# First batch of a fused attention and mixer kernel: the weights e turned in blocks by VectorE and moved by SP, and q and k of five pairs loaded by tokens and turned by TensorE

## The chip, the cores and the metric

The kernel runs on one core of one Trainium2 chip. The time is that of the device in microseconds (us), median of several executions. A profile is one execution, recorded by the hardware; its span is about 2 us shorter than the time. Where a ratio is given, it is the mean time of one kernel's fast runs over the mean of the fast runs of the kernel before in the same rounds on the same chip, so it is not quite the quotient of the medians beside it; the bracket is its 95% interval. The median of the kernel before drifted between 1377.9 and 1380.0 us from one sitting to the next, so small differences are read from the ratios, and two ratios whose intervals overlap are not told apart.

## The reference

```python
scores = q @ k.T / 8                      # 8 batches x 8 heads, 576 tokens, 64 per head
scores = where(scores >= max(scores) - tau, scores, -1e9)
attn   = softmax(scores) @ v              # -> x: 8 x 576 x 512
u      = x + (relu(x.T @ w_tok1) @ w_tok2).T
out    = u + relu(u @ w_ch1) @ w_ch2
```

All is float32; the mixer's weights come as float64 and are converted on the chip while the first two batches run.

## The kernel before

Work is cut into 144 units: a batch has four pairs of heads, two pairs are nine units of 128 query rows (both heads of a pair), so a batch is 18 units. A unit is scores (TensorE), maxima (VectorE), threshold and exponential (ScalarE), normalisation (GpSimd), and then e must be turned so that keys lie on partitions. Three units make a group, whose e is multiplied with v together ("the product"). From the second batch on, the mixer of the batch before runs in TensorE's gaps. The first batch has no such filling, but VectorE, ScalarE and GpSimd convert weights in it.

Each engine takes its instructions in the order in which the program issues them. In a round of the loop over u that order is: scores(u), the product that is due, norm(u-1), weight steps, the turning of unit u-2, weigh(u) (ScalarE), more weight steps, loads, the preparation of the next pair.

```python
def turn(u, third):                       # first batch: by TensorE
    ps = ps_tr.tile(...)                  # PSUM, two buffers, shared with the product
    for c in range(3):
        nc.tensor.transpose(out=ps[:, c, :], in_=e[:, k0 : k0 + P], identity=ident)
    on = nc.scalar.copy if third == 1 and u % 2 else nc.vector.tensor_copy
    on(out=eTs[key][...], in_=ps)

def turn_blocks(u):                       # later batches: 32x32 blocks by VectorE, then moves
    nc.vector.transpose(out=T[:, :, place, :]..., in_=e...)
    if place == GU - 1:                   # the group's last unit
        eT = work.tile([P, GU, 4, NK * 32], F32, tag="eT", bufs=1, name=f"eT_{u}")
        for a in range(4):
            for i in range(4):
                nc.sync.dma_start(out=eT[32*a : 32*a+32, :, i, :], in_=T[32*i : 32*i+32, a, :, :])

def prep(n):                              # q and k of a pair, loaded in 32-wide columns
    nc.vector.transpose(out=sb, in_=src...)   # once for q, once for k

# ...
for x, ps in xs:                          # after the product
    if in_blocks(b): nc.scalar.copy(out=x, in_=ps)
    else: copies.append(lambda x=x, ps=ps: nc.vector.tensor_copy(out=x, in_=ps))
# ...
due.append((u + (2 if in_blocks(wb) else 1), wb, wp, g))   # when the group's product is called
```

## Time and profile before

| | before |
|---|---|
| time | 1378.74 us, 3 runs (1378.43 to 1379.69) |
| span of the profile | 1375.1 us |
| first maxima of unit 0 / 8 / 17 / 18 | 9.4 / 49.0 / 99.8 / 106.2 us |
| x of the first batch starts to be turned ("tx") | 125.4 us |
| from tx to the end | 1249.7 us |

The first batch proper is units 0 to 17. Its x is complete at tx, two units into the second batch, and from there the mixer has work for TensorE. The lines of the profile are in the prediction.

### The profile page before, as it was taken

The page shows a single profiled execution, that of the slowest core. Times are in us where ns is not written, and L with a number is a line of the kernel's source. Part 1 is how long each engine was busy: PE and PEld are TensorE (multiplying, and loading weights), DVE is VectorE, ACT ScalarE, POOL GpSimd, SP SyncE. Part 2 cuts the span into 40 slices and gives each one's busy share as a digit, 9 for nine tenths or more (in the row PEclk, how much of TensorE's full clock was granted, in tenths as well). Part 3 has the DMA queues.
Part 4 walks back from the last instruction along what each step waited for, and adds up shares of the span by engine and source line. Part 5 has one row for each costly group of instructions (what it writes and reads, how often), then busy time and mean ns, then how long its engine had stood idle before and what let it go on. Part 6 is the DMA issues. An engine that isn't in the chain of part 4 may idle for free.

```text
span 1375.1 us, 17691 instructions
## 1 busy us (share of the span) xinstructions
PE 1322.7 (96%) x6226; PEld 817.9 (59%) x6226; DVE 588.2 (43%) x1017; ACT 581.8 (42%) x1288; POOL 356.0 (26%) x683
## 2 busy tenths in 40 slices
PE   6877799999999999999999999999999999999998
PEld 3444465646565666565665567565656576575675
DVE  6788875445444443434244444434333453201000
ACT  5666654454445444443434444353333444120110
POOL 4555653222222222222122222222121222100000
PEclk9988999999999999999999999999999999999999
DMA  5434655454544354433344435434433442400000
GB/s 121 98 96 125 183 142 124 100 123 98 122 109 114 82 121 94 113 88 95 77 100 94 113 77 123 106 83 98 103 87 75 107 103 63 115 1 16 8 11 21
DMA packets 278871, 128.20 MB, mean 93 GB/s; under 512 B 200896, under 2 KB 271552, under 8 KB 278784
## 3 DMA queue, kind: packets, MB, share of 16 engines
q1 hardware_dynamic: 150176, 111.06, 32.0%
q10 hardware_dynamic: 128608, 16.01, 7.3%
q8 instruction: 50, 0.82, 0.3%
q14 instruction: 37, 0.30, 0.1%
HBM read 43.25 MB, written 9.44 MB: 38 GB/s over the span
## 4 chain that ended last, share of the span: by engine, by line
PE 85%; DVE 7%; DMA 2%; SPq 2%; ACT 1%; issue 1%; POOL 1%; ACTq 0%; DVEq 0%; POOLq 0%
PE c L486 26%; PE c L470 26%; PE sc L302 11%; PE pv L413 9%; PE t L441 5%; PE t L448 3%; PE pv L408 3%; DVE mx L307 2%; SPq L374 2%; PE tx L432 1%; PE c L482 1%; DMA eT<-T 1%; PE tr L353 1%; DVE wc L205 1%; ACT e L317 1%
## 5 line engine op out<-in xcount | busy, mean ns | idle before, releaser
L307 DVE TENSOR_REDUCE mx<-sc 128x1 f32<-128x576 f32 x288 | 204.5, 751 | 487.9 <-PE sc L302 487.5
L470 PE MATMUL c<-xT,wc 128*128 128x256 f32 (+1 forms) x1920 | 399.4, 362 | 2.1 <-DVE xT L452 1.2
L486 PE MATMUL c<-wc,g 128*128 128x512 f32 x864 | 390.5, 597 | 0.0
L470 PEld LDWEIGHTS c<-xT,wc 128*128 128x128 f32 x1920 | 334.5, 191 | 71.5 <-issue 27.6
L308 POOL TENSOR_SCALAR bias<-mx,toff 128x1 f32<-128x1 f32 x288 | 82.8, 288 | 799.3 <-DVE mx L307 742.3
L317 ACT ACTIVATE e<-sc,bias 128x576 f32<-128x576 f32 x288 | 199.6, 739 | 162.0 <-POOL bias L308 161.4
L486 PEld LDWEIGHTS c<-wc,g 128*128 128x128 f32 x864 | 157.8, 190 | 175.7 <-issue 174.0
L471 ACT ACTIVATE g<-c 128x256 f32<-128x256 f32 (+1 forms) x240 | 86.7, 362 | 334.1 <-PE c L470 317.9
L324 ACT ACTIVATE e<-e,ntau 128x576 f32<-128x576 f32 x288 | 220.7, 771 | 0.0
L335 POOL TENSOR_SCALAR e<-e,rr 128x576 f32<-128x576 f32 x288 | 215.6, 761 | 15.8 <-DVE rr L332 4.3
L302 PE MATMUL sc<-kT,qT 64*128 64x288 f32 (+1 forms) x1280 | 196.6, 447 | 11.1 <-DVE kT L284 7.1
L365 DVE STREAM_TRANSPOSE T<-e 128x1152 f32<-128x1152 f32 x126 | 172.1, 1366 | 6.3 <-DMA eT<-T 2.6
L302 PEld LDWEIGHTS sc<-kT,qT 64*128 64x128 f32 (+1 forms) x1280 | 107.4, 184 | 98.3 <-issue 59.1
L413 PE MATMUL pv<-eT,lv 128*64 128x384 f32 (+1 forms) x1024 | 136.8, 409 | 0.0
L413 PEld LDWEIGHTS pv<-eT,lv 128*64 128x64 f32 x1024 | 76.1, 138 | 51.0 <-issue 43.6
L491 DVE COPY o<-c 128x512 f32<-128x512 f32 x36 | 24.9, 692 | 177.5 <-PE c L486 177.5
L418 ACT COPY xT<-pv 128x384 f32<-128x384 f32 (+1 forms) x56 | 21.0, 401 | 157.5 <-PE pv L413 157.5
L448 PE MATMUL t<-w,a 128*128 128x288 f32 x256 | 75.2, 421 | 7.2 <-DVE xT L452 5.3
L441 PE MATMUL t<-x_sb,w 128*128 128x512 f32 x160 | 72.1, 598 | 0.0
L448 PEld LDWEIGHTS t<-w,a 128*128 128x128 f32 x256 | 45.6, 191 | 32.2 <-issue 11.4
L452 DVE TENSOR_TENSOR xT<-xT,t 128x288 f32<-128x288 f32 x64 | 28.2, 446 | 80.5 <-PE t L448 80.0
L324 ACT ACTIVATION_READ_ACCUMULATOR e<-e,ntau 128x1 f32 x288 | 56.5, 196 | 0.0
(44 smaller groups left out, 554.7 us busy)
## 6 DMA issues: line engine op xcount, KB each, us to landing
eT<-T SPq DMA_DIRECT2D x672, 108.0 KB, 2.2
scratch<-in_moe_w_ch_dram SPq DMA_DIRECT2D x24, 512.0 KB, 3.7
lv<-in_v_dram SPq DMA_DIRECT2D x32, 288.0 KB, 3.3
out_dram<-o SPq DMA_DIRECT2D x36, 256.0 KB, 2.2
lk<-in_k_dram ACTq DMA_DIRECT2D x111, 72.0 KB, 2.6
lq<-in_q_dram ACTq DMA_DIRECT2D x106, 72.0 KB, 2.3
lq<-in_q_dram SPq DMA_DIRECT2D x22, 72.0 KB, 3.2
lk<-in_k_dram SPq DMA_DIRECT2D x17, 72.0 KB, 3.3
```

The costliest lines, as they stand in the source:

```text
L302: nc.tensor.matmul(sc[h][rows, f, 0:HS], lhsT=qT[r, cols], rhs=kT[r, HS * f : HS * f + HS], start=True, stop=True)
L307: nc.vector.tensor_reduce(out=mx[:, c], in_=sc[h][:, :, 0:HS], axis=AX.XY, op=ALU.max)
L317: nc.scalar.activation(out=eh, in_=sc[h][:, :, 0:HS], func=AF.Prelu, bias=bias[:, h : h + 1], scale=SCALE, alpha=STEEP)
L324: nc.scalar.activation(out=eh, in_=eh, func=AF.Exp, bias=ntau, accum_out=rs[:, h : h + 1])
L335: nc.gpsimd.tensor_scalar(out=eh, in0=eh, scalar1=rr[:, h : h + 1], scalar2=1.0, op0=ALU.mult, op1=ALU.mult)
L365: nc.vector.transpose(out=T[:, :, place, :].rearrange("p a (c x) -> p c a x", c=NK), in_=e.rearrange("p (c a x) -> p c a x", c=NK, a=4))
L413: nc.tensor.matmul(to[r], lhsT=lv[:, j, :], rhs=e[j], start=False, stop=(c == NI - 1), skip_group_check=True)
L441: nc.tensor.matmul(ps, lhsT=w1[:, t, P * m : P * m + P], rhs=x_sb[:, t, :], start=(t == 0), stop=(t == NT - 1))
L448: nc.tensor.matmul(ps, lhsT=s["a"][:, m, P * c : P * c + P], rhs=w2[:, m, HS * f : HS * f + HS], start=(m == 0), stop=(m == NTK - 1))
L470: nc.tensor.matmul(ps, lhsT=wc1[:, j, c, :], rhs=uT[:, c, GR * i : GR * i + n], start=(c == 0), stop=(c == NCC - 1))
L471: nc.scalar.activation(out=s["g"][:, j, 0:n], in_=ps, func=AF.Relu)
L486: nc.tensor.matmul(flat, lhsT=s["g"][:, j, P * t : P * t + P], rhs=wc2[:, j, :], start=False, stop=(j == NJ - 1), skip_group_check=True)
```

## The change

Its intent, as the code shows it: take TensorE's turns, whose PSUM tiles must be emptied by VectorE, out of the first batch, as the later batches already do, and lighten the loads of q and k. It has four parts:

1. Units 0 to 14 are turned in blocks by VectorE and moved by 16 DMAs a group on SP's queue into the one tile eT; the last group (units 15 to 17) is turned by TensorE as before.
2. The product of such a group is called three units after its last turn, not one.
3. The first batch's products are copied from PSUM by ScalarE, not VectorE.
4. q and k of pairs 0 to 4 are loaded with tokens on partitions (256-byte packets, six loads a pair) and turned by TensorE through two PSUM tiles, in place of eight loads of 128-byte packets and a block turn by VectorE.

```diff
+    NATURAL = NP + 1
+    def load_natural(n, eng):
+        for src, t, on in zip((q, k), loaded[n], eng):
+            for h in range(2):
+                on.dma_start(out=t[:, 0:NI, h, :], in_=src[b, 2*p + h, 0:MAIN, :].rearrange("(c t) d -> t c d", t=P))
+            on.dma_start(out=t[0:LAST, NI, :, :], in_=src[b, 2*p : 2*p + 2, MAIN:S, :].rearrange("h t d -> t h d"))
...
-    def in_blocks(b):
-        return b > 0
+    def in_blocks(b, p0, g):
+        return (b, p0, g) != (0, NP - 2, 2)
     def prep(n):
...
-            nc.vector.transpose(out=sb, in_=src.rearrange("p n d -> p (n d)"))
+            for lo, hi in ((0, NI), (NI, NT)):
+                ps = ps_tr.tile([P, MAIN], F32, tag="tr", name=f"{name}{lo}_{n}")
+                for c in range(lo, hi):
+                    nc.tensor.transpose(out=ps[...], in_=src[0:M, c]..., identity=ident[0:M, 0:M])
+                nc.vector.tensor_copy(out=sb[:, P*lo : min(P*hi, S)], in_=ps[...])
...
     # in weigh(u), between threshold and exponential
+        while copies:
+            copies.popleft()()
...
-                copies.append(lambda x=x, ps=ps: nc.vector.tensor_copy(out=x, in_=ps))
+                copies.append(lambda x=x, ps=ps: nc.scalar.copy(out=x, in_=ps))
...
-                due.append((u + (2 if in_blocks(wb) else 1), wb, wp, g))
+                due.append((u + (1 if not blocks else 2 if wb else 3), wb, wp, g))
```

More of the change, by code (lines that the diff above doesn't have):

```diff
@@ L100, in load_qk @@
         if n not in loaded:
-            loaded[n] = [ld.tile([P, S // 32, 32], F32, tag=tag, bufs=1, name=f"{tag}_{n}") for tag in ("lq", "lk")]
+            loaded[n] = [ld.tile([P, NT * 2 * D], F32, tag=tag, bufs=1, name=f"{tag}_{n}")[:, 0:S].rearrange("p (n d) -> p n d", d=32) for tag in ("lq", "lk")]
         for part in parts:
@@ L115, in load_v @@
         vals[n] = lv
+    NATURAL = NP + 1
+    def load_natural(n, eng):
+        b, p = pairs[n]
+        loaded[n] = [ld.tile([P, NT, 2, D], F32, tag=tag, bufs=1, name=f"{tag}_{n}") for tag in ("lq", "lk")]
+        for src, t, on in zip((q, k), loaded[n], eng):
+            for h in range(2):
+                on.dma_start(out=t[:, 0:NI, h, :], in_=src[b, 2 * p + h, 0:MAIN, :].rearrange("(c t) d -> t c d", t=P))
+            on.dma_start(out=t[0:LAST, NI, :, :], in_=src[b, 2 * p : 2 * p + 2, MAIN:S, :].rearrange("h t d -> t h d"))
     vals = {}
@@ L121 @@
         nc.gpsimd.memset(t, 0.0)
-    load_qk(0, (nc.sync, nc.scalar))
+    load_natural(0, (nc.sync, nc.scalar))
     w1 = const.tile([P, NT, DTOK], F32, name="w1")
@@ L283, in prep @@
             sb = work.tile([P, S], F32, tag=name, name=f"{name}_{n}")
-            nc.vector.transpose(out=sb, in_=src.rearrange("p n d -> p (n d)"))
             made.append(sb)
+            if n >= NATURAL:
+                nc.vector.transpose(out=sb, in_=src.rearrange("p n d -> p (n d)"))
+                continue
+            for lo, hi in ((0, NI), (NI, NT)):
+                ps = ps_tr.tile([P, MAIN], F32, tag="tr", name=f"{name}{lo}_{n}")
+                for c in range(lo, hi):
+                    M = MT[c]
+                    nc.tensor.transpose(
+                        out=ps[:, P * (c - lo) : P * (c - lo) + M], in_=src[0:M, c].rearrange("t h d -> t (h d)"), identity=ident[0:M, 0:M]
+                    )
+                nc.vector.tensor_copy(out=sb[:, P * lo : min(P * hi, S)], in_=ps[:, 0 : min(P * hi, S) - P * lo])
         heads[n] = made
@@ L400, in values @@
             ps = whole[:, first : first + N]
-            if in_blocks(b):
+            if in_blocks(b, p0, g):
                 to, e = ps.rearrange("p (m x) -> p m x", x=32), eT[:, first // 32 : (first + N) // 32]
@@ L416, in values @@
         for x, ps in xs:
-            if in_blocks(b):
+            if b:
                 nc.scalar.copy(out=x, in_=ps)
             else:
-                copies.append(lambda x=x, ps=ps: nc.vector.tensor_copy(out=x, in_=ps))
+                copies.append(lambda x=x, ps=ps: nc.scalar.copy(out=x, in_=ps))
     def token_mlp(b):
@@ L541, in values_due @@
             if p0 == NP - 2 and g == 2:
-                if not in_blocks(b):
+                if not b:
                     return True
@@ L560 @@
         last = False
-        if due and not in_blocks(due[0][1]):
+        if due and not due[0][1]:
             last = values_due(u)
@@ L569 @@
             weight_to(2.25 * (u - 1.5))
-        while copies:
-            copies.popleft()()
         if last:
+            while copies:
+                copies.popleft()()
             push(0)
@@ L575 @@
             wb, wp, wt = units[w]
-            if not in_blocks(wb):
+            blocks = in_blocks(wb, wp, wt // GU)
+            if not blocks:
                 for i in range(3):
@@ L582 @@
                     split_middle(wb * NP + wp + g)
-                due.append((u + (2 if in_blocks(wb) else 1), wb, wp, g))
+                due.append((u + (1 if not blocks else 2 if wb else 3), wb, wp, g))
         if b_now:
             fill(0.4)
-        if back and in_blocks(wb):
+        if back and blocks:
             turn_blocks(w)
@@ L605 @@
             if u == 0:
-                load_qk(1, (nc.sync, nc.sync), range(0, 3))
+                load_natural(1, (nc.sync, nc.sync))
             if t in when:
                 m, lo, hi = when[t]
-                if n + m < len(pairs):
+                if n + m < NATURAL:
+                    if lo == 0:
+                        load_natural(n + m, (nc.sync, nc.sync))
+                elif n + m < len(pairs):
                     load_qk(n + m, (nc.scalar if b_now else nc.sync,) * 2, range(lo, hi))
@@ L616 @@
                 prep(n + 2)
-        if due and in_blocks(due[0][1]):
+        if due and due[0][1]:
             values_due(u)
```

## The prediction

> **What bounds the kernel now.** I read the page first: its slices, then its chain, then the busy time of each engine by stage, and at last the order of instructions inside the first batch, the only stage that the change touches. (The program runs 144 units of attention, 18 to a batch; below "unit 8" is the ninth, and a "group" is three units whose turned weights e are multiplied with v together.)
>
> ```profile
> PE   6877799999999999999999999999999999999998
> DVE  6788875445444443434244444434333453201000
> PEclk9988999999999999999999999999999999999999
> ...
> core 0: us, PE busy (x) PEld busy (x) DVE busy (x) ACT busy (x) POOL busy (x), PEclk, DMA share, GB/s
> 7.00:106.20 99.20, 80.80 (x452) 48.77 (x452) 76.89 (x163) 65.66 (x137) 53.48 (x89) 0.91 0.43 99
> 106.20:126.50 20.30, 13.93 (x59) 7.74 (x58) 18.29 (x34) 13.68 (x29) 12.80 (x15) 0.66 0.61 157
> 126.50:200.00 73.50, 62.34 (x302) 40.41 (x303) 63.98 (x95) 46.41 (x97) 44.42 (x51) 0.98 0.58 155
> 200.00:1200.00 1000.00, 994.35 (x4743) 607.45 (x4742) 417.75 (x709) 433.08 (x971) 243.26 (x518) 1.00 0.44 101
> ```
>
> From 200 us on TensorE is busy 99.4% of the time; nothing in the change touches that work. The first batch is 7 to 126 us. No engine is full there: in 7 to 106.2 TensorE has 80.8, VectorE 76.9, ScalarE 65.7 of 99.2 us. So it is bound by engines that wait for each other. The chain of waits says how:
>
> ```profile
> 61.41 2.03 PE sc L302 x8
> 63.45 1.48 PE pv L408 x4
> 64.92 2.71 PE pv L413 x16
> 67.66 0.57 DVE xT L420
> 68.27 1.03 PE tr L353 x6
> ...
> 72.98 0.17 DVE rr L332
> 73.14 0.59 DVE wc L205
> 73.73 0.48 DVE eT L355
> 74.25 0.55 PE tr L353 x3
> 74.80 1.76 PE sc L302 x16
> ```
>
> TensorE turns three blocks, waits for VectorE to empty PSUM, turns the next three, and only then gets to the next scores; VectorE, in its own order, waits for the product with v (67.66) before it can copy it. The groups of VectorE in 7 to 106.2 us size the waits (last columns: idle time before them):
>
> ```profile
> L307 DVE TENSOR_REDUCE mx<-sc 128x1 f32<-128x576 f32 x37 | 26.3, 745 | 8.7 <-PE sc L302 8.4 <-issue 0.2
> L355 DVE COPY eT<-tr 128x384 f32<-128x384 f32 x40 | 21.1, 552 | 4.5 <-PE tr L353 4.5
> L420 DVE COPY xT<-pv 128x384 f32<-128x384 f32 x3 | 1.7, 558 | 6.9 <-PE pv L413 6.9
> L420 DVE COPY xT<-pv 128x192 f32<-128x192 f32 x4 | 1.2, 351 | 0.8 <-PE pv L413 0.8
> ```
>
> Of VectorE's 22.3 us idle, 12.2 (4.5 + 6.9 + 0.8) belong to the turning on TensorE and the copy of the product; about 7 of the 8.4 for scores are start-up, before unit 3. Later batches already move e as the change does in the first, and give its price:
>
> ```profile
> 180.48 10.38 SPq L374 DMA_DIRECT2D eT<-T  x16
> ...
> L365 DVE STREAM_TRANSPOSE T<-e 128x1152 f32<-128x1152 f32 x126 | 172.1, 1366 | 6.3 <-DMA eT<-T 2.6
> ...
> eT<-T SPq DMA_DIRECT2D x672, 108.0 KB, 2.2
> ```
>
> One turn of a unit is 1.37 us of VectorE; the 16 moves of a group are 10.4 us of SP's queue, and the last lands some 2.2 us after its issue.
>
> **What the Trainium skill says.** "VectorE: DVE Perf Modes", The three transpose paths: VectorE turns only 32x32 blocks, a full 128x128 turn is TensorE's and lands in PSUM. Agrees: the block turn has its 16 moves behind it, TensorE's has a copy of 0.55 us per three blocks. "DMA: Bandwidth & Descriptors", Anatomy of one DMA: about 2 us fixed, mostly the receipt of the last byte, and semaphore waits are held by the issuing sequencer, so one waiting DMA holds up all behind it on SP. The landing of 2.2 us agrees; the trace of before shows SP waiting for VectorE's T. "TensorE: Matmul & The Clock Gate", What's actually happening: after an idle window of about 3.4 us the array runs at half clock. Agrees: a unit's scores take 1.17 us in the dense part and 2.0 to 2.3 after pauses (61.41 above), granted clock 0.66 in 106 to 126. "SBUF — State Buffer", Who interferes with whom: two-input VectorE operations and GpSimd reads lock each other out; the weight step of 0.68 us takes up to 1.68 beside GpSimd's. It stays as it is.
>
> **The change part by part.**
>
> 1. Turning of units 0 to 14. VectorE loses 2.5 copies x 0.55 = 1.38 us a unit (ScalarE had one of six), gains one turn of 1.37: nothing. TensorE loses 15 x 9 = 135 turns, about 1.7 us a unit, and the ping-pong with them. ScalarE loses 0.24 a unit. Gain on VectorE's waits: 4.5 us at most.
>
> 2. Copies of the product from VectorE to ScalarE: VectorE loses 1.7 + 1.2 = 2.9 us of work in the window and the 7.7 us of waits. ScalarE, at 66%, takes them at 0.4 to 0.5 us each.
>
> 3. Preparing pairs 0 to 4. Before: two turns, 0.77 + 0.74 = 1.5 us of VectorE. After: ten turns on TensorE and four copies. A PSUM copy of 512 is 0.69 us (the output copy's row), one of 64 about 0.2 (estimate), so 1.78 us of VectorE, +0.28 a pair. Worse is the order: two PSUM tiles, so k's turns wait for q's copies. With four turns at 0.15 us plus 0.1: 0.7 turn, 0.75 copy, 0.7 turn, then 0.7 + 0.2 of copies or the next scores: 3.15 us where TensorE and VectorE take turns. In return a pair's eight loads of 576 packets of 128 B (4608) become six loads with 2304 packets of 256 B: they should land earlier at the start, perhaps by 1.5 us (estimate; the first landed at 5.6 to 5.8 us). Net for pair 0: +0.9 us. Pair 1 at unit 2: +1.6. So unit 4's first maximum, at 26.8 us before, comes at 29.3.
>
> 4. SP. 16 moves x 0.65 = 10.3 us a group, on a queue that had almost nothing to do; plus weights, v and q/k, about 14 us per group. It fits, narrowly.
>
> The new chain in the first batch: there is one buffer eT. A group's moves can't start before the group before has been multiplied. So a round is: 15 issues x 0.65 + 2.2 to the last landing = 12.0 us; product 4.2 us (1.48 + 2.71 above; TensorE comes from a pause, so cold); 0.1 of signalling: **16.3 us** for three units. Before, units 7 to 16 started at 44.0 and 93.1: 49.1 us for nine, 16.4 for three. The new bound is as long as the old one.
>
> Worked through in time: first turned group complete 3.7 us into unit 4, at 33.0 us; moves land 45.0; product ends 49.2; the preparation of pair 2 follows in TensorE's order (+3.15), so unit 8 starts at 52.4 (before 49.0: +3.4). Three rounds later the fourth product ends at 49.2 + 48.9 = 98.1, the preparation of pair 4 follows, unit 17 starts at 101.3 (before 99.8: +1.4). Unit 17 took 6.4 us and loses the wait for the product (0.8), its copies (0.6): 5.0, so unit 18 starts at 106.2, as before. The fifth product ends 114.4, inside unit 18 or 19, which are bound by weights on VectorE (8.5 us each) and unchanged. The last copy on ScalarE need not stand behind VectorE's weights: -0.5. Sum: **-0.5 us**. From there on the program is the same and the shift arrives at the end one to one.
>
> **The rivals.**
>
> A. The waits go and nothing takes their place: VectorE sets the pace. It would save 12.2 us of waits plus 2.9 of work, less 4 x 0.28 of copies and 2.5 at the start: about -11 us, 1368. For: later batches do it so without trouble. Against: their groups have some 27 us (product at 219.05 and 240.87, then 262), those of the first only 16, so the one eT has slack there and not here.
>
> B. The single eT and SP are tighter than I count: a q/k load or a weight piece between the moves (SP stood up to 2.5 us on one load at the start), a move slower with the queues full. Each microsecond costs five times, +5 to +10 us: 1384 to 1389. Against: fewer packets for q and k, and the two units of slack before each preparation.
>
> C. The cold clock: with its turns gone, TensorE pauses longer and scores take 2.3 us. Off the path while VectorE is behind; after each product half of a unit's scores counts, about +0.6 us five times: +3.
>
> D. TensorE's total falls by 135 - 50 = 85 turns. Worth nothing, since it isn't full there.
>
> **Range and chances.** My count gives 1378; the change is visibly fitted to the schedule (the wait of three units, the last group left as it was), so I give A about a third: point **1376**, range **1365 to 1385**. 2% is 27.6 us. All waits of VectorE in the window together are 22.3 us, so faster by 2% is next to impossible (0.02); slower would need five rounds longer by over 5 us each (0.02); within 2% 0.96.
>
> **What would show it.** Right: in 7 to 106 us VectorE's waits for TensorE's turns gone, but new ones before the maxima, behind the product with v; TensorE idle before the product, released by the move of T to eT; the moves waiting for the product; rounds near 16 us; maxima of unit 8 later than 49.0, of unit 18 within 3 us of 106.2; granted clock below 0.91; from 200 us on the same. Wrong: unit 18 at 96 or sooner with VectorE over 85% busy (A), or rounds over 18 us with SP without a gap (B). Also wrong if the saved time were lost again between 126 and 200 us, where weights and SP set the pace.

## The result

| | before | after |
|---|---|---|
| time | 1379.42 us, 6 runs | 1392.82 us, 6 runs (1392.35 to 1394.80) |
| ratio | | 1.0096 (1.0082 to 1.0109) |
| first maxima of unit 0 | 9.4 | 10.8 |
| unit 4 | 26.8 | 30.5 |
| unit 8 | 49.0 | 58.4 |
| unit 17 | 99.8 | 113.8 |
| unit 18 | 106.2 | 119.4 |
| tx | 125.4 | 141.5 |
| from tx to the end of the profile | 1249.7 | 1251.4 |

The change costs 13.4 us, about 1%. The two profiles lie 17.8 us apart, more than the medians: that of before is of an execution of 1376.9 us, faster than any timed one, that of after of the slowest, 1394.8.

The slices and the busy times by stage after, with the same columns as before:

```profile
PE   7667899999999999999999999999999999999998
...
7.00:106.20 99.20, 71.88 (x271) 40.70 (x271) 70.07 (x128) 60.16 (x125) 51.55 (x83) 0.86 0.63 159
119.40:140.00 20.60, 14.71 (x80) 8.73 (x82) 17.87 (x33) 11.74 (x24) 12.76 (x15) 0.75 0.78 198
140.00:215.00 75.00, 64.50 (x306) 40.84 (x304) 62.87 (x91) 45.69 (x92) 44.70 (x50) 0.95 0.57 151
215.00:1215.00 1000.00, 994.82 (x4746) 607.19 (x4743) 419.10 (x710) 435.37 (x977) 245.68 (x519) 1.00 0.43 100
```

(The granted clock of 0.86 from 7 to 106 us, and the 0.91 of before, are too high: the record of the clock begins only at 54.5 us in this profile, at 24.1 in that of before, and the table counts what is not recorded as full clock. The last section comes back to this.)

In the same 99.2 us every compute engine did less than before: VectorE 70.1 us in place of 76.9, ScalarE 60.2 in place of 65.7. So no engine became the bound; the engines wait longer for each other. Only the DMA engines are busier, 0.63 in place of 0.43. The dense part from 215 us on is as it was. What VectorE waited for from 7 to 119 us, before (first fence) and after (columns: who waited for whom, us in total, times, longest; the stretch is the same, but the changed kernel is one unit behind in it):

```profile
DVE mx L307 <- PE sc L302: 8.4, 8, 2.4
DVE xT L420 <- PE pv L413: 7.7, 4, 2.9
DVE eT L355 <- PE tr L353: 6.0, 14, 1.0
```

```profile
DVE mx L329 <- PE sc L324: 16.4, 11, 3.8
DVE qT L307 <- PE qT L304: 13.4, 2, 8.8
DVE kT L307 <- PE kT L304: 4.5, 5, 1.1
```

The two waits that the change aimed at (the product, the turns) are gone, 13.7 us; 34.3 us stand where 22.1 stood. The chain of waits after shows the new loop (start, us, what):

```profile
46.28 2.23 DMA eT<-T
48.51 0.30 issue
48.81 1.55 PE pv L431 x4
50.36 4.70 PE pv L436 x16
55.06 0.60 PE qT L304 x4
...
84.20 2.32 DMA eT<-T
86.52 0.24 issue
86.76 1.54 PE pv L431 x4
88.30 4.52 PE pv L436 x16
92.84 0.64 SPq L397
```

Read it downwards: the last of 16 moves lands, the product runs, behind it in TensorE's order comes the preparation of a pair, and at 92.84, the moment the product ends, SP issues the next group's first move, which had been held back by the one eT. The moves themselves, on SP's queue, with the loads between them (start, us, how many):

```profile
73.27 11.54 SPq L397 DMA_DIRECT2D eT<-T  x16
84.92 0.52 SPq L188 DMA_DIRECT2D scratch<-in_moe_w_ch_dram  x1
85.53 1.06 SPq L126 DMA_DIRECT2D lq<-in_q_dram  x2
86.65 0.65 SPq L127 DMA_DIRECT2D lq<-in_q_dram  x1
87.40 1.09 SPq L126 DMA_DIRECT2D lk<-in_k_dram  x2
88.53 0.64 SPq L127 DMA_DIRECT2D lk<-in_k_dram  x1
```

The products start at 48.8, 67.5, 86.8 and 105.0 us: rounds of 18.7, 19.2 and 18.2 us for three units, where the kernel before took 16.4.

### The profile page after: what moved, and what is told of

Its sections match the earlier page's. It is cut to its first block, busy times and chain, and to the rows that moved or that the text cites. A ratio compares the mean times of both kernels' runs of the same rounds, so it can differ in the third digit from the quotient of the medians.

```text
span 1392.9 us, 17563 instructions
## 1 busy us (share of the span) xinstructions
PE 1332.4 (96%) x6141; PEld 819.3 (59%) x6141; DVE 588.0 (42%) x996; ACT 583.2 (42%) x1289; POOL 361.3 (26%) x683
## 4 chain that ended last, share of the span: by engine, by line
PE 86%; DVE 5%; SPq 3%; DMA 3%; ACT 1%; issue 1%; POOL 0%; ACTq 0%; DVEq 0%; POOLq 0%
PE c L509 27%; PE c L493 25%; PE sc L324 11%; PE pv L436 9%; PE t L464 5%; PE t L471 3%; SPq L397 3%; PE pv L431 3%; DVE mx L329 2%; PE tx L455 1%; PE c L505 1%; DMA scratch<-in_moe_w_ch_dram 1%; DMA eT<-T 1%; ACT e L339 1%; DVE T L388 1%
## 5 line engine op out<-in xcount | busy, mean ns | idle before, releaser
L493 PEld LDWEIGHTS c<-xT,wc 128*128 128x128 f32 x1920 | 333.9, 190 | 71.9 <-issue 27.6
L324 PE MATMUL sc<-kT,qT 64*128 64x288 f32 (+1 forms) x1280 | 210.0, 456 | 14.7 <-ACT e L339 14.2
L388 DVE STREAM_TRANSPOSE T<-e 128x1152 f32<-128x1152 f32 x141 | 192.7, 1367 | 6.6 <-DMA eT<-T 3.4
L324 PEld LDWEIGHTS sc<-kT,qT 64*128 64x128 f32 (+1 forms) x1280 | 115.2, 188 | 110.3 <-issue 60.8
L436 PE MATMUL pv<-eT,lv 128*64 128x384 f32 (+1 forms) x1024 | 143.4, 424 | 0.0
L436 PEld LDWEIGHTS pv<-eT,lv 128*64 128x64 f32 x1024 | 79.6, 144 | 54.8 <-issue 48.3
L431 PE MATMUL pv<-eT,vl 128*64 128x384 f32 (+1 forms) x256 | 48.2, 455 | 13.4 <-DMA eT<-T 12.0
```

The lines of the kernel that those rows point to most:

```text
L324: nc.tensor.matmul(sc[h][rows, f, 0:HS], lhsT=qT[r, cols], rhs=kT[r, HS * f : HS * f + HS], start=True, stop=True)
L388: nc.vector.transpose(out=T[:, :, place, :].rearrange("p a (c x) -> p c a x", c=NK), in_=e.rearrange("p (c a x) -> p c a x", c=NK, a=4))
L431: nc.tensor.matmul(to[r], lhsT=vl[:, r], rhs=e[NI], start=True, stop=False, skip_group_check=True)
L436: nc.tensor.matmul(to[r], lhsT=lv[:, j, :], rhs=e[j], start=False, stop=(c == NI - 1), skip_group_check=True)
L493: nc.tensor.matmul(ps, lhsT=wc1[:, j, c, :], rhs=uT[:, c, GR * i : GR * i + n], start=(c == 0), stop=(c == NCC - 1))
```

## The experiments

Each is an edit of the changed kernel unless it says "the kernel before". Fifteen were run. One gives a wrong result (no loads of pairs 2 to 4, under "Is it the loads?"); all others were correct.

### One part of the change at a time

**Only the copies on ScalarE** (the kernel before with part 3).

```diff
-                copies.append(lambda x=x, ps=ps: nc.vector.tensor_copy(out=x, in_=ps))
+                copies.append(lambda x=x, ps=ps: nc.scalar.copy(out=x, in_=ps))
```

> The kernel before with only the third part of the change: the copies of the first batch's product go from VectorE to ScalarE. If VectorE's wait for the product (7.7 us) and its copies (2.9 us) are on the path: -5 us or better, near 1374. Rival, the wait only moves on to the scores that stand behind the turns in TensorE's order: within 2 us of 1379.4.

Measured: 1379.79 us, ratio 1.0003 (0.9977 to 1.0030). The rival's number holds: 7.7 us of waits for the product were worth nothing. They moved on, but to the turns more than to the scores: in this run's profile VectorE waits 17.3 us for TensorE's turns (6.0 before) and 9.9 for scores (8.4 before), from 7 to 119 us (its tx starts at 129.6 us, 4.2 later than in the profile of before, though the times agree). A wait that another takes over is not a gain.

**Only q and k by tokens** (the kernel before with part 4).

```diff
-    load_qk(0, (nc.sync, nc.scalar))
+    load_natural(0, (nc.sync, nc.scalar))     # and so for pairs 1 to 4; prep() through TensorE for them
```

> The kernel before with only the second part of the change: q and k of five pairs loaded by tokens and turned by TensorE; e turned by TensorE as before. If every preparation costs by its exchange between TensorE and VectorE: +3.7 us until unit 3 and about +1.9 us for each of the other three, +9 us, near 1388. If the preparations cost only at the start: +3.7, near 1383. If the lighter loads were worth something: 1379 or less.

Measured: 1391.72 us, ratio 1.0085 (1.0057 to 1.0112). By the median dearer than any of the three expectations, but the first of them (9 us, a ratio of 1.0065) lies inside the interval. It is the same as the whole change within the intervals. The start and pair 1 cost 5.0 us (unit 4 at 31.8 us), pair 2 with the unit behind it another 4.2 (unit 9 is 9.2 late), pair 3 hardly anything (unit 16 is 9.8 late), pair 4 with the unit behind it 4.1 (unit 18 is 13.9 late). VectorE waits for TensorE's turns of q and k (6.8 us in all), and the scores and products behind them in TensorE's order come later (13.1 and 10.4 us of waits, 8.4 and 7.7 before).

**All but q and k by tokens** (part 4 undone).

```diff
-    NATURAL = NP + 1
+    NATURAL = 0                                # loads and preparation of all pairs as before
```

> The changed kernel with q and k of all pairs loaded and turned as before (VectorE's block turn), only e moved by SP. Theory of the serial round: the round of moves and product does not contain the preparation, so rounds stay at 18 to 19 us, and only the start (unit 4 earlier by 3.7 us) and the last preparation behind a product (3.3 us before unit 17) are won: -7 us, near 1386. Rival 1, each of the four preparations is fully on the path: -12 us, near 1381. Rival 2, the fine packets of 128 B and two more issues a pair hold up SP and the moves: no gain, 1391 or more.

Measured: 1391.92 us, ratio 1.0093 (1.0063 to 1.0123). The start was won as expected (unit 4 at 27.6 us, not 30.5), and unit 8 came 7.7 us sooner than in the changed kernel, but at the preparation of pair 3 all was lost again: the eight fine loads stood on SP's queue, some before and the last two behind the third group's moves (69.1 to 79.4 us).

```profile
81.65 0.78 DVE L298 STREAM_TRANSPOSE qT<-lq 128x576 f32<-128x576 f32 x1 [9.02 <-issue]
83.02 0.78 DVE L298 STREAM_TRANSPOSE kT<-lk 128x576 f32<-128x576 f32 x1 [0.59 <-DMA lk<-in_k_dram]
```

The bracket is VectorE's idle time before the instruction: 9.0 us. The view names no releaser for it ("issue"), but the trace has the last load of q landing at 81.57 us, just before the turn starts. So parts 1 and 4 belong together in this schedule: with the moves on SP, the old loads come too late; with the new loads, the preparations cost TensorE and VectorE an exchange. The costs don't add: each half alone is as slow as the whole.

### The loops: one buffer, and three units of lag

**Two buffers eT** (the second lies in the tile of the channel mixer, unused in this batch).

```diff
-            eT = work.tile([P, GU, 4, NK * 32], F32, tag="eT", bufs=1, ...)
+            eT = work.tile([P, GU, 4, NK * 32], F32, tag="g" if b == 0 and (u // GU) % 2 else "eT", bufs=1, ...)
```

> The changed kernel with two buffers eT in the first batch (the second lies in a tile that is not used there). Theory, one eT makes a serial round of moves (12 us) plus cold product (5.4 to 6.3 us): with two buffers the moves start when VectorE has turned the group, rounds of products fall from 18.2-19.2 us to about 15 (then TensorE's order and SP's 14 us bind), unit 17 starts some 9 us earlier, total near 1384. Rival, SP's queue is full anyway (moves plus loads of q, k, v and weights): rounds stay over 18 us and the total over 1390.

Measured: 1392.55 us, ratio 1.0104 (1.0077 to 1.0130): no gain, and my theory that the one eT alone sets the round fell. The second group's moves did start at 48.7 us, not at 55.1, but the products still started at 49.4, 66.2, 84.3 and 103.0 us. TensorE stands before them all the same where the moves come late, as here before the fourth:

```profile
102.97 1.55 PE L431 MATMUL pv<-eT,vl 128*64 128x384 f32 x4 [3.65 <-DMA eT<-T]
104.28 5.09 PE L436 MATMUL pv<-eT,lv 128*64 128x384 f32 x16
```

The second theory: two loops of like length. One goes through eT. The other goes through the lag: turn, moves, product, and behind the product in TensorE's order the next scores, which feed the next turns. With three units of lag and some 4.3 us a unit there are 13 us for moves of 12 and a product of 5 to 6.

**Lag of four units, one eT**, and **lag of four units, two eT**. (The fifth group keeps three, so as not to delay the end of the batch.)

```diff
-                due.append((u + (1 if not blocks else 2 if wb else 3), wb, wp, g))
+                due.append((u + (1 if not blocks else 2 if wb else 3 if wp and g == 1 else 4), wb, wp, g))
```

> The changed kernel with the product called four units after a group's last turn, not three (the fifth group keeps three); one eT. Two eT alone gave nothing: products still came 16.8 to 18.7 us apart. Theory: two loops of like length run side by side, the one through the single eT (moves 12 us, product 6) and the one through TensorE's order (turn, moves, product, then the scores behind it, three units on). A longer lag opens only the second: the products stay over 17.5 us apart and the total within 3 us of 1392.8. Rival, the lag alone is what is too short: total 1387 or less.

> Two eT and four units of lag, so both loops open. Theory: TensorE no longer stands before its products, VectorE's waits of 9 us at unit 7 and 5 us at unit 16 shrink to the preparations' own 3 us, unit 18 comes near 110 us, total near 1383. Rival, SP and the loads are the limit (moves start late behind loads): total stays over 1389.

Measured: 1390.32 us, ratio 1.0085 (1.0057 to 1.0113), and 1384.97 us, ratio 1.0045 (1.0023 to 1.0068).

| | lag three | lag four |
|---|---|---|
| one eT | 1392.8 | 1390.3 |
| two eT | 1392.6 | 1385.0 |

Either alone wins 0 to 2.5 us, both win 7.8; by the ratios it is -1 to 1.5 and 7. Only the gain of both is clear of the intervals. That is what two loops side by side look like. The products' lines say the same; with one eT TensorE still waits for the moves (2.69 us before the third product), with two it doesn't:

```profile
86.97 1.55 PE L431 MATMUL pv<-eT,vl 128*64 128x384 f32 x4 [2.69 <-DMA eT<-T]
88.27 4.58 PE L436 MATMUL pv<-eT,lv 128*64 128x384 f32 x16
```

```profile
82.54 1.55 PE L431 MATMUL pv<-eT,vl 128*64 128x384 f32 x4
83.87 4.24 PE L436 MATMUL pv<-eT,lv 128*64 128x384 f32 x16
```

### Is it the loads?

In the version with both loops open the moves of the groups began 12.6, 17.9, 18.3 and 12.5 us apart, and the two long distances are those with loads of q and k between. So I took SP's issues for the limit that was left.

**Loads of pairs 2 to 4 issued by ScalarE**, in the changed kernel and with both loops open.

```diff
-                        load_natural(n + m, (nc.sync, nc.sync))
+                        load_natural(n + m, (nc.scalar, nc.scalar))
```

> The changed kernel (one eT, lag three) with the loads of q and k of pairs 2 to 4 issued by ScalarE, not SP. In the trace SP issues 10.4 us of moves and then 6 to 8 us of loads in a round of 18. If SP's issues alone set the round, it falls to 13-15 us and the total to 1385 or less. If the loop through the one eT (12 us of moves, 6 of cold product) is as long as SP's, the products stay 17.5 to 18.5 us apart and only the 2 us before the first move are won: 1389 to 1392.

> As before with two eT and four units of lag, but the loads of q and k of pairs 2 to 4 issued by ScalarE. With both loops open SP was the limit that was left: its moves began 12.6 us apart where no loads lay between and 17.9 and 18.3 us where they did. Theory: with the loads away the moves follow VectorE's turns, 13 to 15 us apart, and the total falls from 1385 to about 1380; what is left to 1378 is the preparations by TensorE. Rival: nothing is won, 1384 or more.

Measured: 1396.58 us, ratio 1.0126 (1.0102 to 1.0151), and 1389.52 us, ratio 1.0070 (1.0050 to 1.0090). Both are slower than with the loads on SP (ratios 1.0096 and 1.0045), by 3 to 4 us; each interval overlaps that of its partner, so it is the two together, and the traces, that speak for a loss. The moves of the third group, in the changed kernel 11.5 us (above), took, with the loads on the other queue:

```profile
73.95 17.32 SPq L397 DMA_DIRECT2D eT<-T  x16
```

SP's queue stood, as its own waits show, until a load of q landed, though ScalarE had issued it (8.0 us in two waits, the longest 5.2):

```profile
SPq L397 <- DMA lq<-in_q_dram: 8.0, 2, 5.2
```

Why should a move of e wait for a load of q? The trace shows the semaphores: in this run all DMAs, of both queues, tell of their landing through the same eight (numbers 100 to 107), used again and again, and a DMA waits until the one that used its semaphore before has landed. The move at 89.33 us waits for number 102, whose last user was a load of q that ScalarE issued at 86.68 and that landed at 89.32. So it is not shown that the transfers themselves hold each other up; the program ties the two queues together, and SP waits until ScalarE gets to its loads.

**No loads of pairs 2 to 4** (both loops open; pair 1's are used again, so the result is wrong).

```diff
+        if n > 1:
+            loaded[n] = loaded["kept"]          # pair 1's tiles
+            return
```

> The version with two eT and lag four (1385), with the loads of q and k of pairs 2 to 4 left out (pair 1's are used again: a wrong result on purpose). Theory: moves and loads together set the rounds of 18 us there, so the first moves of groups follow each other by 12.5 to 14.5 us throughout, and the total falls to 1378 to 1382. Rival, the rounds of 18 us come from the preparations or the products: the starts of moves stay 17 us or more apart in rounds two and three, total 1384 or more.

Measured: 1384.88 us, ratio 1.0036 (1.0009 to 1.0064), beside 1.0045 with the loads. The rival holds and my reading of the distances falls: with no load between, the moves still began at 47.6, 65.7, 83.4 and 95.9 us. SP mostly waited there. The long rounds are those with a preparation in them: VectorE took 9.0 us from unit 11 to unit 12, where pair 3 is prepared, and 3.6 to 4.6 us for the units beside it. In this version no cost of the loads on SP is to be seen: the two ratios differ by 0.0009, well within their intervals.

### The clock

**Ten idle products a unit** (128 x 128, behind the scores of units 3 to 17, into a PSUM tile that nobody reads).

```diff
             scores(u)
+            if b_now == 0 and u > 2:
+                warm = ps_tr.tile([P, MAIN], F32, tag="tr", name=f"warm_{u}")
+                for _ in range(10):
+                    nc.tensor.matmul(warm[:, 0:P], lhsT=ident, rhs=ident, start=True, stop=True)
```

> The changed kernel with ten idle 128x128 products on TensorE behind the scores of units 3 to 17, into a PSUM tile that nobody reads: nothing is taken away, only the clock should stay up. If the half clock of the product is part of the round: the product takes 3.4 to 4.5 us in place of 5.4 to 6.3, and the total falls by 3 to 6 us in spite of 15 to 25 us more work on TensorE. Rival, the clock is off the path or TensorE is full: no gain, or a loss.

Measured: 1389.57 us, ratio 1.0073 (1.0045 to 1.0102), against 1.0096 without. By the ratios that is a gain of some 3 us, at the lower end of what was expected, but the intervals overlap, so the gain in time is not shown. What the traces show is the product. The stretches of the second to fourth product, first of the changed kernel, then with the idle products (stretch, its length, TensorE's busy time first; third number from the end: the granted clock):

```profile
67.52:72.96 5.44, 5.44 (x42) 4.51 (x42) 2.85 (x6) 1.48 (x2) 3.12 (x5) 0.63 0.93 236
86.76:92.80 6.04, 6.04 (x22) 2.43 (x22) 5.10 (x8) 1.94 (x3) 4.82 (x7) 0.56 0.89 226
104.97:110.45 5.48, 5.47 (x21) 2.26 (x22) 1.49 (x2) 0.28 (x1) 1.82 (x4) 0.62 0.53 183
```

```profile
68.32:71.79 3.47, 3.47 (x43) 2.85 (x42) 2.35 (x6) 1.31 (x2) 2.70 (x4) 1.00 1.15 287
86.45:89.90 3.45, 3.44 (x22) 1.65 (x22) 2.79 (x3) 0.00 (x1) 3.22 (x4) 1.00 0.98 247
104.79:108.24 3.45, 3.45 (x21) 1.66 (x22) 0.00 (x0) 0.00 (x0) 0.00 (x0) 1.00 0.87 299
```

The same work takes 3.45 us in place of 5.4 to 6.0, so the half clock is shown to be what the product cost. But the rounds stayed at 18 to 19 us: what the product no longer took was taken up by the next moves, which started 0.9 to 1.6 us after it and in the last round lasted 1.9 us longer. (The first product, after the longest pause, still took 6.3 us.) A term can be mis-sized and its repair hardly come out at the end, if a second loop is just as long.

**The kernel before with the same idle products**, as the control.

> The kernel before with only the ten idle products behind the scores of units 3 to 17. There TensorE is 81% busy and its turns are on the path, so 1.5 us more work a unit should cost: 1380 to 1388. Rival, the clock is all that the best version gained by: 1374 or less.

Measured: 1393.81 us, ratio 1.0096 (1.0072 to 1.0120), a loss, larger than expected: the ten products took 2.5 us, not the 1.5 I had put down, and they stand in front of the turns on which VectorE waits (13.9 us from 7 to 120 us, where it was 6.0; the waits for the product behind them rose from 7.7 to 16.5 us). The clock by itself is no gain here, where TensorE's own work is on the path.

### A version that is faster than both

**All mended**: two eT, lag four, q and k loaded and turned by VectorE as before the change, their loads in the first batch issued by ScalarE.

```diff
-                    load_qk(n + m, (nc.scalar if b_now else nc.sync,) * 2, range(lo, hi))
+                    load_qk(n + m, (nc.scalar,) * 2, range(lo, hi))
```

> Two eT, four units of lag, q and k loaded and turned by VectorE as before the change, and their loads of the first batch issued by ScalarE so that SP has only moves, weights and v. Theory: the waits that the change brought in are all gone; VectorE sets the pace at 4.3 to 4.8 us a unit, unit 18 comes near 96 us (106.2 before), total near 1369. Rival, something else takes the place (ScalarE's issues, the cold clock of the scores): 1377 or more.

Measured: 1378.20 us, ratio 0.9996 (0.9973 to 1.0019). The loss of the change is all recovered, but the gain that I expected is not there: unit 18 starts at 103.5 us, 2.7 us sooner than before, not 10. VectorE still waited for scores behind products of 5.7 and 6.2 us, 2.9 us for the loads of pair 3, and 4.4 us for TensorE's turns of the first of the last group's units.

**All mended, with the idle products**, twice, the second time with more rounds:

> The mended version (two eT, lag four, q and k as before the change, loads on ScalarE; 1378.2) with the ten idle products a unit. VectorE waited 2.4 and 3.3 us behind products of 5.9 and 6.2 us at half clock. Theory: products take 3.4 to 4.5 us, total near 1373. Rival, those idle products stand in the way of the scores or the turns of the last group: 1378 or more.

> The best version once more, unchanged: 1371 to 1374 if the 0.58% is real.

Measured: 1372.74 us, ratio 0.9942 (0.9916 to 0.9969), and 1373.50 us, ratio 0.9951 (0.9926 to 0.9975). It is clearly faster than the kernel before, by half a per cent; the same version without idle products was not (0.9996). The first four products take 3.4 to 3.5 us, the granted clock is 1.00 from 25 us, where its record begins, to 100 us, and tx starts at 122.5 us (125.4 before).

**The same with the loads of pair 3 issued at once**, three units ahead:

```diff
+                if n == 0 and t == 8:
+                    hi = 8                      # all eight parts, not three
```

> As the one before, and the loads of q and k of pair 3 all issued at unit 8, three units before they are turned, where VectorE waited 2.9 us for them at unit 11. Expected: another 2 to 3 us, near 1371; if ScalarE's issues (4 us at once) hold up its exponentials, no gain.

Measured: 1376.80 us, ratio 0.9976 (0.9956 to 0.9996): still just faster than the kernel before, but by its middle worse than without the edit (0.9942, and 0.9951 in the repetition), though the intervals overlap. Unit 11 starts at 64.8 us, 5.8 us later than in the first run without this edit, and unit 12 at 71.8, 4.6 later. ScalarE's issues in one block may be the cause; no run separates them from the burst of packets.

## Why the prediction was wrong

The direction was left open. Most of the signs that it named came: the waits for turns gone, new ones behind the product, TensorE idle until the last move lands, the moves waiting for the product. But the rounds, which it put near 16 us, took 18 to 19: one term of them was mis-sized, and the loop that it counted is not the only one. Point by point:

**VectorE's work doesn't change** (step 1): right. Fifteen turns at 1370 ns took the place of copies, and the exchange of TensorE and VectorE for them went away.

**The copies** (step 2): the work left VectorE as said, but the 7.7 us of waits were no gain, as the run with the copies alone shows.

**The preparations** (step 3): 3.15 us behind a product was right at the one place where it was counted (55.07 to 58.35 us: 3.28). The start was put too low: unit 4 was to start at 29.3 and started at 30.5.

**The first moves** were to start at 33.0 us. The turn ended at 34.1, and SP then had the loads of pair 2, a weight piece and v in front of the moves, from 31.8 to 36.4: they started at 36.45, another 2.3 us late.

**The round of 16.3 us** is the step that failed, and in it the term "product 4.2 us". The moves were right (36.45 to 48.5: 12.1 us). The products took 6.3, 5.4, 6.0 and 5.5 us. I had taken 4.2 from the kernel before, where TensorE comes to the product from its turns, and had called that cold; but in that product the half clock ended at 65.0 us, 1.6 us after its start. After the change the turns are gone and the product runs at half clock nearly throughout. The prediction itself named this (rival C), but charged it to the scores only. From the end of the first product to the end of the fourth, 48.9 us were predicted and 55.4 measured: 4.4 of the 6.5 us are products, 2.0 are moves that took 12.4 and 13.5 us to the product's start. Together with the start (1.2), the late first moves (2.3), the first product (2.1) and 0.3 of signalling and preparation this is 12.4 us, and unit 17 started at 113.75 us, not at 101.3. This says where the time lay, not what mending one term would win: with the product at full clock (idle products, above) the rounds still took 18 to 19 us.

**The end of the batch** was to gain 0.5 us. It lost: the fifth product starts at 125.7 us, so TensorE's turns of the last group and the scores of unit 20 come behind it; unit 20 starts 13.5 us late and tx 16.1.

**From there on** the program is the same, and the shift arrives at the end: right.

**The rivals.** B (SP and the one eT tighter than counted, 1384 to 1389) came nearest by its number, and even that was too low. Its reason was not the right one: SP was not full, as its moves waited 12.2 us in two waits for TensorE (30 to 128 us), and leaving out the loads won nothing that the intervals show. The weight of a third that I gave to A, because the change looked fitted to its schedule, drew the middle from 1378 to 1376 and the top of the range to 1385; the trace spoke against it, as the prediction itself said (some 27 us for a later group, 16 for these). The plain count, 1378 with five uncertain rounds around it, was the better centre, though its terms were too small as well.

**The second step that failed**: the prediction treated the loop through eT as the only one. The two-by-two table shows a second, through the lag of three units; the preparations by TensorE are a third cost, 6.8 us between the version with both loops open and the one that also has q and k as before (1385.0 and 1378.2). That comparison also cuts the loads as before and moves them to ScalarE; the move of the loads by itself lost 3 to 4 us by the ratios in the two runs that tried it, so it hardly is what won. Two things stay open: how much of those 6.8 us is the exchange through PSUM and how much the place in TensorE's order, and why pairs 2 and 4 cost over 4 us each in the kernel before, where the count gave 1.9, and pair 3 almost nothing.

## What to carry to other kernels

When a transfer replaces an engine's work, count the whole loop that it closes, with the buffer that comes free last and the engine that stands in order behind it, and look for a second loop of the same length before mending the first: here one buffer and one unit of lag were each worth almost nothing and together 7 to 8 us. Taking work from TensorE may slow what is left on it; take the duration of a step from a stage whose clock and neighbours are those of the new schedule, not the old. Half an improvement that needs the other half (moves on one queue, loads on the same) can cost as much as both. And a transfer that is put on another queue is not free of the first as long as the program gives both the same semaphores.

## What the Trainium skill lacked or had wrong

- "TensorE: Matmul & The Clock Gate", Part 1, What's actually happening, ties the half clock to an idle window of about 3.4 us. The length agrees: but for one cut off at the end, every recorded stretch at half clock in the profile of before is a whole multiple of 3.41 us. The idleness doesn't: the stretches in which the second to fourth product ran after the change began at 61.3, 85.2 and 98.9 us, and within the 3.4 us before each TensorE was idle for at most 1.0, 0.8 and 1.2 us at a stretch. (The half clock at 61.41 us that the prediction took for agreement followed a pause of 3.0 us.) Under A second HAM failure mode the same page does tell of a kernel in which short idles had this effect. How much work is enough neither says: 3.41 us in which TensorE was busy 74% (from 81.8 us) were followed by half clock, and 3.41 us with 55% (from 115.9) were not.
- The same page, under Seeing it yourself, warns that the clock's trace events can be unreliable. What misled here was simpler, a record that begins late (54.5 us after the change, 24.1 before) and is counted as full clock until then: the first product after the change took 6.26 us, about as long as the others at half clock, in a stretch that the table gives as 1.00. Durations decide.
- The same page, Part 4 (PE-mode transpose), says that the full clock doesn't engage for TensorE's transposes. Here the turns of 128x128 float32 ran at both clocks: in the kernel before they followed each other by 110 ns (median) where the recorded clock is full and by 214 where it is half. The trace calls them MATMUL and doesn't show whether the transpose mode was on; whether turns alone raise the clock no run shows.
- "DMA: Bandwidth & Descriptors", Issuing engines are not separate DMA queues, says that issuing from several engines saves only the sequencer's time. That isn't contradicted here, but it doesn't mention what can be lost: 16 moves on SP took 17.3 us where the program let them share eight semaphores with loads issued by ScalarE, 11.5 with the loads on SP itself.
- For what one such copy costs the issuing sequencer, that page has only 512 cycles for "previous generations", in a table on trn3, without naming trn2 or a clock. Here a move of 32 partitions took 0.60 us of SP's queue (0.585 at least), 0.65 from one start to the next, so that 16 of them are 10.4 us.
